# A gated pair of S4 convolutions on one core: cheaper seeds, gates and Dskip, and u's transform split 64 x 32

## The chip, the cores and the metric

The kernel runs on one NeuronCore of a Trainium2 chip. The metric is device time in microseconds of one execution, from the runs' own timer; the profile's span (first to last instruction) is about 2 us shorter. The engines are PE (matmul, with its weight loads listed as PEld), DVE (vector), ACT (activation functions and copies), POOL (a second elementwise engine) and SP, which issues DMAs. Each has its own instruction queue, worked off strictly in order; they meet through semaphores.

## The reference

Two state space layers, A and B, each with 512 channels and 128 complex states, filter the same input u (2048 x 512), and a gate per time step mixes the results:

```python
P = exp(dt * A[:, :, None] * l)                  # 512 x 128 states x 2048 steps, complex
K = einsum("dn,dnl,dn->dl", C, P, dt * B).real   # one kernel of 2048 taps per channel
y = irfft(rfft(u, 4096) * rfft(K, 4096))[:2048] + u * Dskip   # causal convolution
g = sigmoid((u * gate_w).sum(-1, keepdims=True))
out = g * y_A + (1 - g) * y_B
```

## The kernel before, in words

All arithmetic is fp32. The 512 channels are worked in 8 chunks (c) of 64; a chunk holds both layers, so 128 columns. The kernel K of a chunk comes in 8 groups of 16 columns: 64 table steps T in all.

*Preparation.* `exp_dt` and `prep` (three groups of chunks: 0, then 1 to 3, then 4 to 7) turn A, B, C and dt into a magnitude, a phase and their logarithms per state and column. PE transposes them with a diagonal matrix, built from an identity in the constant tile `small`.

*Seeds and tables.* `seed(c)` fills two small tiles per chunk: `ml` (exp of al times 0..7 and times 0, 8, .. 56) and `mh` (exp of al times 0, 256, .. and 0, 64, 128, 192), one ACT instruction of 128 columns for every power, 25 a chunk, with the column of ones set by memset once. `seed_angles` does the phases on POOL. Each `tables(T)` multiplies seeds into magnitudes `mr` (POOL, some on DVE) and angles `ang` (POOL), takes sines on ACT (`s`, `sq`), makes `ei` and `mr` real and imaginary parts on DVE, and then PE's `kgen` (L593) contracts over the states: 32 matmuls, each with 32 weight columns in one of four column tiles of PE and 64 columns moved. ACT or DVE copies the 64 x 4 taps from PSUM to `kt`. After every second step POOL adds Dskip (tile `dsk`, zero except in the rows of tap 0) to tap 0 in `kt` (L599), and `first` (L610) begins the transform of the pair.

*Transforms.* A length of 2048 is split as 32 rows (stride 64) times 64. `first` contracts over the 32 rows for four column groups at once, 16 matmuls of 64 weight columns by 128 moved, and writes `xa` or `xb`; `spectrum` (L623) contracts over the 64 with full 128 x 128 matmuls whose weights `w2` (2 MB) stay in SBUF. u goes through the same two functions, in four batches (`u_spectra`, 4 calls of `first` and 8 of `spectrum` each), and its spectrum is stored to DRAM (`us`). `conv` multiplies the spectra on DVE, `back` does the inverse (L714, 64 x 64 tiles of PE) and turns the result over DRAM (`z` to `zb` to `f`, for the last chunk to `xa`), and `fin` (L745) does its last matmuls with the gates as weights, copies to `o` (two buffers) and stores.

*Gates.* `gated` lets PE multiply u with `gate_w`, copied to all 128 rows by a broadcast weight (L655, 4 groups), copies the result, applies Tanh once over 2048 columns on ACT, and scales it in place against the transform's cosines: two DVE operations (L671) and one on POOL (L674) for each of four groups. The result `gsi` holds the weights of `fin`.

*Order.* Every operation gets a number as the program is recorded by `Plan`, with engines it may run on. The table `ORDER` lists all numbers in the order in which they are issued (a "b" picks the second engine). So the order on each engine is fixed by hand or by a planner beforehand, not found at run time. Buffers are rings: 4 PSUM banks `c`, 2 `s`/`sq`, 3 `u`, 2 `uin`, 2 `o`. A helper makes each kind of operation, so many of the profile's lines are those of helpers: L276 (tensor_tensor), L286 (scalar_tensor_tensor), L289 (activation), L294 (DMA), L299 and L301 (copies on ACT and on DVE).

Of the kernel before, what the change touches and what calls it, by code (L numbers as in the profile page):

```python
# [45 lines left out]
def constants():  # L46
    f32 = np.float32
    out = {}
    l1, f1, l2, f2 = np.arange(L1), np.arange(F1), np.arange(L2), np.arange(F2)
    b, g1, a, g2 = np.arange(NB), np.arange(G1), np.arange(NA), np.arange(G2)  # L50
# [3 lines left out]
    for q in range(4):  # L54
# [6 lines left out]
    out["w2"] = np.ascontiguousarray(w2.transpose(1, 0, 2)).reshape(128, F1 * 128).astype(f32)  # L61
    ang = 2 * np.pi * ((b[:, None] * (4 * g1[None, :] + 1)) % 256) / 256
# [8 lines left out]
    out["small"] = np.concatenate([w1.reshape(128, 256), si, si / 2, np.eye(128),  # L71
                                   np.full((128, 1), math.pi / 4)], 1).astype(f32)
# [10 lines left out]
4 182 183 2 0 1 186 82 3 18 19 20 21 22 23 25 26 27 28 29 24 30 31 32 33 34 88 35 185b 184 37 38 40 44 36 39 41 42 47 46 76 11  # L83
399 79 369 43 8 9 12 7 45 48 49 51 50 138 187 188b 86 190 191 74 71 72 53 52 193 189b 84 13 367 83 85 87 222 14 16 194 192b 55
54 56 57 91 92 73 58 61 62 75 94 93 95 59 96 60 63 64 65 89 68 67 69 90b 70 98 101 100 99 102 103 105 104 195 223 66 77 370 78
371 373 114 196b 197b 198 374 107 375 199 113 201 224b 10 372 376 377 378 382 97 80 383 384 400 6 385 81 401 202 379 15 226
204 205 106 108 109 207 208 200 203 210 213 209 206 211b 110 225 386 214 380 381 216 217 219 220 111 389 112 115 116 390 121
122 123 124 117 118 119 227 342 230 215 212 221 234 127 126 129 231 387 229 388 228 431 432 235 403 391 404 233 392 393 120
433 402 412 413 232b 414 415 236 237b 250 394 405 251 218 128 125 406 407 408 409 253 259 256 410 254b 257b 416 417 418 260 17
411b 419 420 421 134 136 132 244 247 368 130 141 131 144 137 262 255 252 5 422 142 143 245b 248b 145 146 135 258 133 343 261  # L90
266 148 150 151 149 152 492 495 491 493 494 445 429 443 430 446 444 395 498 434 139 154 163 153 155 164 437 438 423 241 238
239b 140 435 436 424 157 447 242 156 439 440 158 450 159 451 396 397 448 398 449 147 460 425 461 462 463 426 441 428 427 442
263 452 453 160 464 465 264 466 265 454 455 161 473 475 474 476 162 467 267 165 166 468 268 477 478 469 269b 470 171 172 173
174 480 481 1413 499 344 270 240 274 175 249 246 243 176 346 347 271 272b 273b 167 168 169 275 276b 277b 471 479 623 625 627
# [112 lines left out]
def ssm_mix(ctx: ExitStack, tc: tile.TileContext, a, out, dry=False):  # L207
# [641 lines left out]
```

## Time and profile before

| | |
|---|---|
| time, median of 3 runs | 453.33 us (450.59 to 453.42) |
| the profiled execution's own time | 454.36 us |
| its span | 452.3 us |
| busy: PE, DVE, ACT, POOL | 397.1 (88%), 406.6 (90%), 379.6 (84%), 358.6 (79%) us |
| DMA moved | 84.56 MB, mean 187 GB/s |
| mean granted PE clock | 0.991 |

A row of a group names the line, the engine, the operation, its output and inputs with shapes, then the count, the busy time, the mean ns of one, and the idle time of the engine just before with what ended it. In rows of PE a form such as `128*32 128x64` means 128 rows, 32 weight columns, 64 columns moved. A matmul of the code appears as two passes. Busy time of many short overlapping instructions is counted once, so count times mean can be more than the busy time. The chain is the sequence of work and waits followed back from the last instruction.

### The profile page before, as it was taken

What the parts mean: (1) busy time and instruction counts of PE and PEld (TensorE: products, weight loads), DVE (VectorE), ACT (ScalarE), POOL (GpSimd) and SP (SyncE); (2) the same over time, 40 slices, a digit from 0 to 9 for tenths busy, and PEclk for the clock granted to TensorE, in tenths of its full rate; (3) what the DMA queues carried; (4) which work ended last, traced back from release to release, by engine and by line L of the source; (5) the groups of instructions that cost most, each with busy time, mean ns of one, the idle gap of its engine ahead of it and who ended that gap; (6) DMA issues with size and microseconds to landing.
All of it is one profiled execution on the core that took longest, in us unless ns stands there. A gap on an engine that the chain in (4) does not pass through costs nothing.

```text
span 452.3 us, 22101 instructions
## 1 busy us (share of the span) xinstructions
PE 397.1 (88%) x9628; PEld 354.7 (78%) x9628; DVE 406.6 (90%) x517; ACT 379.6 (84%) x656; POOL 358.6 (79%) x328
## 2 busy tenths in 40 slices
PE   5798967899998878998998998988998889989994
PEld 4787866788886767897988888877887778888973
DVE  5899999999989999899999999999999998986720
ACT  3778899999897999899999999999999978884120
POOL 0795968799988789999999899889999998980010
PEclk9979999999999999999999999999999999999999
DMA  6728942738646567577456554674466857756785
GB/s 205 246 80 266 291 157 77 229 86 260 234 142 194 171 195 214 159 227 214 135 163 186 177 158 143 196 233 114 132 193 197 234 170 203 241 156 190 213 245 152
DMA packets 79760, 84.56 MB, mean 187 GB/s; under 512 B 7728, under 2 KB 62256, under 8 KB 79664
## 3 DMA queue, kind: packets, MB, share of 16 engines
q1 hardware_dynamic: 79472, 82.63, 61.3%
q8 instruction: 75, 1.23, 1.1%
q0 software_dynamic: 192, 0.52, 0.3%
q14 instruction: 21, 0.17, 0.1%
HBM read 51.48 MB, written 31.65 MB: 184 GB/s over the span
## 4 chain that ended last, share of the span: by engine, by line
PE 39%; DVE 20%; ACT 17%; issue 10%; DMA 8%; POOL 4%; SPq 1%; DVEq 0%; ACTq 0%; POOLq 0%
PE c L623 11%; PE c L610 10%; PE c L593 6%; DVE mr L286 5%; PE c L745 4%; PE c L714 4%; DVE ei L276 3%; ACT s L289 3%; DVE y L694 3%; ACT ang L289 3%; DMA out_dram<-o 3%; PE c L655 2%; ACT sq L289 2%; DMA zb<-z 2%; ACT L289 2%
## 5 line engine op out<-in xcount | busy, mean ns | idle before, releaser
L286 DVE SCALAR_TENSOR_TENSOR mr<-sq,mr 128x1024 f32<-128x1024 f32 (+1 forms) x128 | 117.0, 949 | 2.7 <-ACT sq L289 2.4
L276 POOL TENSOR_TENSOR mr<-ml 128x1024 f32<-128x1024 f32 x52 | 101.6, 1954 | 9.1 <-PE c L593 6.5
L276 DVE TENSOR_TENSOR ei<-s,mr 128x1024 f32<-128x1024 f32 x64 | 77.8, 1216 | 1.4 <-POOL mr L276 0.6
L593 PE MATMUL c<-mr 128*32 128x64 f32 x2048 | 64.0, 222 | 15.3 <-DVE mr L286 5.3
L276 POOL TENSOR_TENSOR ang<-par,cint 128x512 int32<-128x512 int32 x64 | 67.6, 1057 | 10.1 <-ACT sq L289 10.0
L694 DVE TENSOR_TENSOR y<-c,u 128x1024 f32<-128x1024 f32 x57 | 68.3, 1216 | 3.8 <-PE c L623 2.8
L610 PE MATMUL c<-small,kt 128*64 128x128 f32 x1024 | 64.4, 276 | 7.3 <-issue 3.4
L276 POOL TENSOR_TENSOR mr<-mh 128x512 f32<-128x512 f32 x64 | 68.5, 1075 | 1.1 <-PE c L593 0.8
L289 ACT ACTIVATE s<-ang 128x1024 f32<-128x1024 int32 x64 | 66.1, 1032 | 3.3 <-DVE ei L286 2.6
L276 POOL TENSOR_TENSOR ang<-sa 128x512 int32<-128x512 int32 x64 | 68.6, 1073 | 0.2
L289 ACT ACTIVATE ang<-ang 128x1024 f32<-128x1024 int32 x64 | 67.7, 1058 | 1.2
L289 ACT ACTIVATE sq<-ang 128x1024 f32<-128x1024 f32 x64 | 66.2, 1035 | 2.7 <-DVE mr L286 1.8
L593 PEld LDWEIGHTS c<-mr 128*32 128x32 f32 x2048 | 48.3, 109 | 25.3 <-issue 9.0
L610 PEld LDWEIGHTS c<-small,kt 128*64 128x64 f32 x1024 | 56.0, 137 | 12.3 <-issue 7.0
L593 PE MATMUL c<-ei 128*32 128x64 f32 x2048 | 63.0, 219 | 0.5 <-issue 0.5
L714 PE MATMUL c<-y,vv 64*64 64x128 f32 x1792 | 59.2, 273 | 2.3 <-ACT kt L299 0.7
L714 PEld LDWEIGHTS c<-y,vv 64*64 64x64 f32 x1792 | 50.7, 133 | 8.0 <-issue 2.1
L623 PE MATMUL c<-xa,w 128*128 128x128 f32 x384 | 52.5, 284 | 4.9 <-DVE vv L419 2.2
L623 PEld LDWEIGHTS c<-xa,w 128*128 128x128 f32 x384 | 45.8, 191 | 9.7 <-issue 3.6
L623 PE MATMUL c<-xb,w 128*128 128x128 f32 x384 | 50.5, 282 | 2.7 <-DVE xb L301 1.9
L593 PEld LDWEIGHTS c<-ei 128*32 128x32 f32 x2048 | 50.2, 110 | 0.8 <-issue 0.6
L623 PEld LDWEIGHTS c<-xb,w 128*128 128x128 f32 x384 | 45.2, 191 | 6.3 <-DVE xb L301 1.6
(110 smaller groups left out, 653.4 us busy)
## 6 DMA issues: line engine op xcount, KB each, us to landing
zb<-z SPq DMA_DIRECT2D x64, 256.0 KB, 3.4
u<-us SPq DMA_DIRECT2D x57, 256.0 KB, 3.9
f<-zb SPq DMA_DIRECT2D x112, 128.0 KB, 3.7
us<-z SPq DMA_DIRECT2D x32, 256.0 KB, 3.6
uin<-in_uk_dram SPq DMA_DIRECT2D x16, 256.0 KB, 3.2
f<-in_ut_dram SPq DMA_DIRECT2D x8, 512.0 KB, 5.1
out_dram<-o SPq DMA_DIRECT2D x28, 128.0 KB, 2.6
par<-prd SPq DMA_DIRECT2D x7, 320.0 KB, 4.1
```

The lines of the kernel that those rows point to most:

```text
L276: lambda e: (dve if e == "dve" else pool).tensor_tensor(out=out(), in0=in0(), in1=in1(), op=o),
L286: lambda _: dve.scalar_tensor_tensor(out=out(), in0=in0(), scalar=s, in1=in1(), op0=o0, op1=o1), reads, writes, port=port)
L289: op("act", "act", n, lambda _: act.activation(out=out(), in_=in_(), func=func, **{k: v() if callable(v) else v for k, v in kw.items()}), ...
L593: pe.matmul(ps[32 * j:32 * j + 32, o], x[:, 4 * o + j, 64:96], x[:, 4 * o + j, 0:64], start=part == 0, stop=part == 1, tile_position=(0, 3 ...
L610: pe.matmul(t(*ps[g // 4])[64 * r:64 * r + 64, 128 * (g % 4):128 * (g % 4) + 128], t(*x)[:, g], t("small")[:, 128 * r:128 * r + 128], star ...
L623: pe.matmul(view()[:, :, k], t("w2", j // 2)[:, 4 * (j % 2) + k], t(*x1)[:, 4 * j + k], start=True, stop=True)
L655: pe.matmul(p[:, 2 * n:2 * n + 2], t("gate_w")[:, k:k + 1].to_broadcast([128, 128]), fv(n)[:, :, k], start=k == 0, stop=k == 3)
L694: op("dve", "tt1", 1024, lambda _: dve.tensor_tensor(out=t(*y).rearrange("p h s f d -> p h s (f d)"), in0=fv().rearrange("p s f d -> p s ( ...
L714: pe.matmul(bank_of(x)[64 * e:64 * e + 64, CH * q:CH * q + CH], v[:, 0:64] if h else v[:, 32:96], t(*ys[f // 4])[64 * x:64 * x + 64, h, :, ...
L745: pe.matmul(t(*ps)[64 * r:64 * r + 64, DC * i:DC * i + DC], t("gsi")[:, 4 * k + i, s, 64 * r:64 * r + 64], t(*f)[:, 8 * k + 2 * i + r, DC ...
```

## The change

- *Seeds.* POOL multiplies al with the row 0..7 into `ml` (one operation of 1024 elements), and four ACT instructions make all powers of a chunk from it, three of 1024 and one of 512 elements, written in runs of 8 or 4. The memsets go.
- *Dskip.* After each table step DVE adds `dsk` to the tap 0 that it reads from PSUM, 4 elements a row, and writes it to `kt`, behind the copy. POOL's add after every second step goes.
- *u's transform.* 64 rows (stride 32) times 32. `first_u`: 64 matmuls a call, 32 weight columns in four column tiles, 64 columns moved. `spectrum_u`: 16 matmuls a call for two of the old calls, in 64 x 64 tiles, with weights `w2u` loaded from DRAM for each of four groups of a batch into the ring `u` (16 loads of 256 KB). The order of the frequencies f1 in the constants changes with it.
- *Gates.* PE's product with `gate_w` goes to 32 rows in four column tiles (32 matmuls in two calls), Tanh reads it from PSUM in two calls of 256 columns, four matmuls of 512 columns spread a row to all 128 rows, and DVE makes both halves of `gsi` from PSUM (16 operations of 256 elements). The identity and the cosines lie in `o` for a time.
- *The end.* The last two outputs of the last chunk go to `uin` buffers instead of `o`; the second queue for output DMAs is ACT's, not POOL's.
- *Order.* The whole table `ORDER` is another one. Besides the operations above, 9 copies to `kt`, 8 of the output copies of `fin`, 16 to `xa` and `xb` and 7 to `z` move from DVE to ACT, and two products of tables from POOL to DVE.

At the start of PE's queue the first transforms of u (`uin`) and the second ones (`xb`) stand as follows before; `ei` with `y` or `gsi` are the transposes of the preparation.

```order
L610 MATMUL c<-small,uin 64x128 x16
L444 MATMUL c<-ei,y 128x128 x5
L610 MATMUL c<-small,uin 64x128 x32
L444 MATMUL c<-ei,gsi 128x128 x15
L610 MATMUL c<-small,uin 64x128 x32
L623 MATMUL c<-xb,w_0_195 128x2x64 x8
L623 MATMUL c<-xb,w_1_196 128x2x64 x8
L623 MATMUL c<-xb,w_2_197 128x2x64 x8
```

And so in the changed kernel, where L647 is `first_u` and L664 `spectrum_u`, whose weights lie in `u`:

```order
L647 MATMUL c<-small,uin 32x64 x64
L459 MATMUL c<-ei,y 128x128 x4
L647 MATMUL c<-small,uin 32x64 x64
L459 MATMUL c<-ei,y 128x128
L647 MATMUL c<-small,uin 32x64 x64
L459 MATMUL c<-ei,gsi 128x128 x15
L647 MATMUL c<-small,uin 32x64 x64
L664 MATMUL c<-xb,u 64x2x64 x32
L647 MATMUL c<-small,uin 32x64 x64
L664 MATMUL c<-xb,u 64x2x64 x32
L647 MATMUL c<-small,uin 32x64 x64
```

A call of 16 matmuls became one of 64, 32 matmuls of L664 stand for 16 of the old full-size ones, and six calls of the first transform instead of five stand ahead of the first `kgen`.

In the middle of the program, POOL's queue before holds the Dskip add of a pair among its table products (`kt`, the number names the buffer's instance):

```order
L276 TENSOR_TENSOR mr_3410<-mh_1_194 128x16x32
L276 TENSOR_TENSOR ang_3587<-par_1869,cint_201 128x16x32
L276 TENSOR_TENSOR ang_3587<-sa_2930 128x16x32
L276 TENSOR_TENSOR mr_3594<-mh_1_194 128x16x32
L276 TENSOR_TENSOR kt_3458<-kt_3458,dsk_2630 128x8
L276 TENSOR_TENSOR ang_3598<-par_1869,cint_201 128x16x32
L276 TENSOR_TENSOR ang_3598<-sa_2930 128x16x32
```

In the changed kernel it is DVE's queue that holds two adds for the pair, each reading the bank `c` of its own table step, among the products of tables (`ei`, `mr`) and of the convolution (`y`):

```order
L291 TENSOR_TENSOR ei_3834<-s_3745,mr_3718 128x16x64
L301 SCALAR_TENSOR_TENSOR ei_3834<-s_3745,mr_3718 128x16x32
L743 TENSOR_TENSOR y_3848<-c_3842,u_3821 128x1024
L743 TENSOR_TENSOR y_3862<-c_3857,u_3829 128x1024
L291 TENSOR_TENSOR kt_3840<-c_3748,dsk_3134 128x4
L301 SCALAR_TENSOR_TENSOR mr_3718<-sq_3855,mr_3718 128x16x64
L743 TENSOR_TENSOR y_3954<-c_3866,u_3825 128x1024
L291 TENSOR_TENSOR kt_3840<-c_3871,dsk_3134 128x4
L301 SCALAR_TENSOR_TENSOR mr_3718<-sq_3855,mr_3718 128x16x32
```

The add moved from POOL to DVE and from one per pair to one per step; what stands behind it there are the products `mr` and `y`.

The diff, cut to its core:

```diff
 ORDER = """
-4 182 183 2 0 1 186 82 3 18 19 20 21 22 23 25 26 27 28 29 24 30 31 32 33 34 88 35 185b 184 37 38 40 44 36 39 41 42 47 46 76 11
...
+174 2 4 175 13 14 15 16 17 18 20 21 22 23 24 25 19 26 27 28 0 5 29 80 3 9 178 8 1 182 74 76 75 30 177 31 176 78 32 33 34 39 35
...
-    def dma(size, out, in_, reads, writes, also_pool=False, touch=()):
-        op("sp pool" if also_pool else "sp", "dma", size,
-           lambda e: (sp if e == "sp" else pool).dma_start(out=out(), in_=in_()), reads, writes, touch=touch)
+    def dma(size, out, in_, reads, writes, also_act=False, touch=()):
+        op("sp act" if also_act else "sp", "dma", size,
+           lambda e: (sp if e == "sp" else act).dma_start(out=out(), in_=in_()), reads, writes, touch=touch)
...
-    def seed(c, parts):
+    def seed(c):
         ml, mh = ("ml", c % 2), ("mh", c % 2)
-        cols = [(mh, l, 256 * l) for l in range(1, 8)] + [(mh, 8 + l, 64 * l) for l in range(4)]
-        cols += [(ml, l, l) for l in range(1, 8)] + [(ml, 8 + l, 8 * l) for l in range(1, 8)]
...
-                        act.activation(out=t(*tile)[:, ks, j], in_=t("par", c)[:, 0, ks].bitcast(F32), func=AF.Exp, scale=float(l))
...
+        tt("pool", CH * 8, lambda: t(*ml)[:, :, 0:8], lambda: t("par", c)[:, 0].bitcast(F32).unsqueeze(2).to_broadcast([128, CH, 8]),
+           lambda: t("small")[:, 513:521].unsqueeze(1).to_broadcast([128, CH, 8]), OP.mult, par(c, "al") + [("small",)], q[0])
+
+        def exps(_):
+            x = t(*ml)
+            for o, n, l in ((t(*mh)[:, :, 0:8], 8, 256), (t(*mh)[:, :, 8:12], 4, 64), (x[:, :, 8:16], 8, 8), (x[:, :, 0:8], 8, 1)):
+                act.activation(out=o, in_=x[:, :, 0:n], func=AF.Exp, scale=float(l))
...
+        tt("dve", 4, lambda: t(*kt)[:, 4 * (T % 2):4 * (T % 2) + 4, 0], lambda: t(*kc)[:, 0:256].rearrange("p (o l) -> p o l", o=4)[:, :, 0],
+           lambda: t("dsk", c)[:, g], OP.add, [kc, kt, ("dsk", c)], [kt], port=False)
         if T % 2:
-            tt("pool", 8, lambda: t(*kt)[:, :, 0], lambda: t(*kt)[:, :, 0],
-               lambda: t("dsk", c)[:, g - 1:g + 1].rearrange("p t o -> p (t o)"), OP.add, [kt, ("dsk", c)], [kt])
...
+    def first_u(b, h, x, x1):
...
+            for g in range(16):
+                for r in range(4):
+                    pe.matmul(t(*ps[g // 8])[32 * r:32 * r + 32, 64 * (g % 8):64 * (g % 8) + 64], xv[:, g],
+                              t("small")[:, 256 + 64 * r:320 + 64 * r], start=True, stop=True, tile_position=(0, 32 * r))
...
+    def spectrum_u(b, J, x1):
+
+        w, ps = ("u", "w2u", b, J), [("c", "us", b, 2 * J + x) for x in range(2)]
+        dma(256, lambda: t(*w).rearrange("p h f d -> p (h f d)"), lambda: a["w2u"][:, 512 * J:512 * J + 512], (), [w])
+
+        def mm(_):
+            for m in range(4):
+                for x in range(2):
+                    for e in range(2):
+                        pe.matmul(t(*ps[x])[64 * e:64 * e + 64].rearrange("p (h f d) -> p h f d", h=2, f=4)[:, :, m],
+                                  t(*w)[64 * x:64 * x + 64, e, m], t(*x1)[64 * x:64 * x + 64, 8 * J + 4 * e + m],
+                                  start=True, stop=True, tile_position=(64 * x, 64 * e))
...
+                for k in range(4):
+                    for n in range(4):
+                        pe.matmul(t(*ps)[32 * n:32 * n + 32, 0:256].rearrange("p (i l) -> p i l", i=2),
+                                  t("gate_w")[:, k:k + 1].to_broadcast([128, 32]), fv(n)[:, :, k], start=k == 0, stop=k == 3,
+                                  tile_position=(0, 32 * n))
...
+            actv(256, lambda P=P: t(*gt)[:, 4 * P:4 * P + 4].rearrange("p a l -> p (a l)"), lambda ps=ps: t(*ps)[:, 0:256], AF.Tanh,
+                 [ps], [gt] * (P == 0) + [("tanh", P)], table=0, scale=0.5, touch=[gt] * (P > 0))
...
+                pe.matmul(t(*ps), t("small")[:, 521 + n:522 + n].to_broadcast([128, 128]), t(*gt).rearrange("p a l -> p (a l)"),
+                          start=True, stop=True)
...
+                        dve.scalar_tensor_tensor(
+                            out=t("gsi")[:, 8 * P + 2 * n:8 * P + 2 * n + 2, s],
+                            in0=t(*ps)[:, 256 * P:256 * P + 256].rearrange("p (i l) -> p i l", i=2), scalar=1.0,
+                            in1=t("o", "si").rearrange("p a l -> p (a l)")[:, 128 * s:128 * s + 128].unsqueeze(1).to_broadcast([128, 2, 128]),
+                            op0=o, op1=OP.mult)
...
-        f, ps, o = home(c), ("c", "fin", c, k), ("o", c, k)
+        late = c == NCH - 1 and k >= 2
+        f, ps, o = home(c), ("c", "fin", c, k), ("uin", "late", k) if late else ("o", c, k)
```

More of the change, by code (lines that the diff above doesn't have):

```diff
@@ L61, in constants @@
     out["w2"] = np.ascontiguousarray(w2.transpose(1, 0, 2)).reshape(128, F1 * 128).astype(f32)
+    g = (f1.reshape(4, 2, 1, 4).transpose(1, 0, 2, 3) + F1 * np.arange(2)[:, None]).reshape(2, F1)
+    ang = 2 * np.pi * ((np.arange(64)[:, None, None] * (4 * g + 1)) % 256) / 256
+    c, s = np.cos(ang), np.sin(ang)
+    w1u = np.zeros((2, 64, 2, 2, F1, 2))
+    for q in range(2):
+        w1u[q, :, :, 0, :, q] = c
+        w1u[q, :, :, 1, :, q] = -s
+    k = np.arange(32)[None, :, None, None] * (4 * g[:, None, :, None] + 1 + 256 * g2)
+    ang = 2 * np.pi * (k % 8192) / 8192
+    c, s = np.cos(ang), np.sin(ang)
+    w2u = np.stack([np.stack([c, -s], 4), np.stack([s, c], 4)], 1)
+    out["w2u"] = w2u.reshape(128, F1 * 64).astype(f32)
     ang = 2 * np.pi * ((b[:, None] * (4 * g1[None, :] + 1)) % 256) / 256
@@ L643, in gated @@
     def gated():
-        for h in range(4):
-            ps, w, f = ("c", "rows", h), ("gsi", h), ("f", "gate", h // 2)
-            fv = lambda n, f=f, h=h: t(*f)[:, 16 * (h % 2) + 8 * n:16 * (h % 2) + 8 * n + 8].rearrange("p (i k) l -> p i k l", i=2)
-            for n in range(2):
-                dma(512, lambda n=n, fv=fv: fv(n), lambda n=n, h=h: a["ut"][:, 4 * h + 2 * n:4 * h + 2 * n + 2], (),
-                    [f, ("gated", h, n)])
-            def mm(_, ps=ps, fv=fv):
-                p = t(*ps).rearrange("p (i l) -> p i l", i=4)
-                for n in range(2):
-                    for k in range(4):
-                        pe.matmul(p[:, 2 * n:2 * n + 2], t("gate_w")[:, k:k + 1].to_broadcast([128, 128]),
-                                  fv(n)[:, :, k], start=k == 0, stop=k == 3)
-            op("pe", "gate", 32, mm, [f, ("gated", h, 0), ("gated", h, 1), ("gate_w",)], [ps], table="full")
-            copy(512, lambda h=h: t("gsi")[:, 4 * h:4 * h + 4, 0], lambda ps=ps: t(*ps).rearrange("p (i l) -> p i l", i=4), [ps],
-                 [w] + R(1, "P0", "P1", "P2", "P3", "B0", "B1"))
@@ L661, in gated @@
[L661 to L674 removed]
+        dma(128, lambda: t("o", "si").rearrange("p a l -> p (a l)"), lambda: a["si"], (), [("o", "si")])
@@ new lines, in gated, with mm, scaled @@
+        for n in range(4):
+            ps, w = ("c", "rows", n), ("gsi", n)
+            def mm(_, ps=ps, n=n):
+                pe.matmul(t(*ps), t("small")[:, 521 + n:522 + n].to_broadcast([128, 128]), t(*gt).rearrange("p a l -> p (a l)"),
+                          start=True, stop=True)
+            op("pe", "rows", 8, mm, [("tanh", 0), ("tanh", 1), ("small",)], [ps], table="full", touch=[gt])
+            for s, o in ((0, OP.add), (1, OP.subtract)):
+                def scaled(_, s=s, o=o, ps=ps, n=n):
+                    for P in range(2):
+                        dve.scalar_tensor_tensor(
[3 more added lines that the diff above has]
+                            op0=o, op1=OP.mult)
+                op("dve", "stt2", 512, scaled, [ps, ("o", "si")], [w] + R(1, "P0", "P1", "P2", "P3", "B0", "B1"), port=False)
@@ L764, in ssm_mix @@
     load("cint")
-    load("small", 257)
+    load("small", 263)
+    dma(64, lambda: t("o", "eye").rearrange("p a l -> p (a l)")[:, 0:128], lambda: a["eye"], (), [("o", "eye")])
     load("gate_w")
     memset("dummy", lambda: t("dummy"))
-    for k in range(2):
-        for n, j in (("mh", 0), ("ml", 0), ("ml", 8)):
-            memset(n, lambda n=n, j=j, k=k: t(n, k)[:, :, j], *((n, k, q) for q in range(CH // QK)))
     for k in range(4):
@@ L775, in ssm_mix @@
     prep(0)
-    seed(0, ((0, CH),))
+    seed(0)
     seed_angles(0, ((0, 32), (32, 96)))
```

170 lines of the change are left out of this document (75 added, 95 removed), and 49 rows, old and new, of the table ORDER.

## The prediction

> **What bounds the kernel now.** I read the table of stretches first (busy time of each engine), then the chain of waits, then the groups of instructions, and last the single rows of the chain at the start and at the end. The columns of the stretches are length, then busy us of PE, PE's weight loads, DVE, ACT and POOL, the granted clock, the DMA share and GB/s.
>
> ```profile
> core 0: us, PE busy (x) PEld busy (x) DVE busy (x) ACT busy (x) POOL busy (x), PEclk, DMA share, GB/s
> 0.00:30.00 30.00, 21.88 (x201) 19.84 (x202) 23.26 (x63) 18.88 (x42) 14.58 (x22) 0.89 0.59 183
> 30.00:60.00 30.00, 25.74 (x429) 24.17 (x430) 28.78 (x39) 25.07 (x53) 24.42 (x23) 1.00 0.87 258
> ...
> 100.00:140.00 40.00, 38.89 (x888) 34.65 (x882) 38.62 (x46) 37.23 (x55) 37.34 (x34) 1.00 0.69 216
> ...
> 410.00:437.00 27.00, 26.72 (x681) 24.77 (x682) 14.62 (x17) 7.41 (x15) 0.92 (x2) 1.00 0.74 212
> 437.00:452.00 15.00, 9.51 (x140) 6.04 (x138) 1.21 (x4) 1.16 (x3) 1.62 (x3) 0.96 0.62 184
> ...
> 30.00:410.00 380.00, 338.94 (x8608) 304.03 (x8608) 367.46 (x437) 352.16 (x597) 341.45 (x302) 1.00 0.62 186
> ...
> PE 39%; DVE 20%; ACT 17%; issue 10%; DMA 8%; POOL 4%; SPq 1%; DVEq 0%; ACTq 0%; POOLq 0%
> ```
>
> The reader should see three stages. From 30 to 410 us all four engines are nearly full, DVE most of all: 367.46 of 380, 96.7%, against 92.7% for ACT and 89-90% for POOL and PE. After 410 PE works alone; after 437 the end waits for transfers. The chain jumps between engines (PE 39%, DVE 20%, ACT 17%), so nothing is won by relieving one engine only; in the middle the time follows DVE's load as long as the others lose as much.
>
> **ACT, part by part.** The seeds, the table loads and the copies out of PSUM have these rows (busy us, mean ns of one):
>
> ```profile
> L528 ACT ACTIVATE ml<-par 128x128 f32<-128x128 f32 x112 | 29.4, 431 | 0.1
> L528 ACT ACTIVATE mh<-par 128x128 f32<-128x128 f32 x88 | 23.8, 439 | 0.1
> L528 ACT ACT_TABLE_LOAD x12 | 15.4, 1283 | 0.2
> L289 ACT ACTIVATE s<-ang 128x1024 f32<-128x1024 int32 x64 | 66.1, 1032 | 3.3 <-DVE ei L286 2.6 <-POOL ang L276 0.5
> L299 ACT ACTIVATE z<-c 128x512 f32<-128x512 f32 x67 | 38.0, 593 | 7.8 <-PE c L623 3.4 <-DMA zb<-z 1.7 <-PE c L714 1.5
> L299 ACT ACTIVATE kt<-c 128x256 f32<-128x256 f32 x45 | 17.2, 381 | 7.3 <-PE c L593 7.3
> L289 ACT ACTIVATE gsi<-gsi 128x2048 f32<-128x2048 f32 x1 | 1.9, 1912 | 0.0
> ```
>
> Removed: 200 exponentials, 29.4 + 23.8 = 53.2; table loads fall from 29 to 21 in the instruction order, 8 x 1.283 = 10.3; the Tanh 1.9 and two copies of gates 1.2: 66.6. Added: eight seeds of three 1024-wide and one 512-wide pass, 8 x (3 x 1.032 + 0.593) = 29.5. The new order also gives ACT copies that were DVE's: 23 more of 512 at 0.593, 19 more of 256 at 0.381 (two of these are the new Tanh), one of 384 at about 0.5: 21.3. Net -15.8. [...]
>
> **DVE.**
>
> ```profile
> L301 DVE COPY z<-c 128x512 f32<-128x512 f32 x21 | 14.0, 683 | 3.1 <-DMA f<-zb 2.0 <-PE c L714 0.8 <-PE c L623 0.3
> L301 DVE COPY kt<-c 128x256 f32<-128x256 f32 x19 | 7.8, 418 | 1.7 <-PE c L593 1.5
> L671 DVE SCALAR_TENSOR_TENSOR gsi<-gsi,small 128x256 f32<-128x256 f32 x8 | 8.0, 1057 | 0.0
> L286 DVE SCALAR_TENSOR_TENSOR ea<-ea,er 128x8 f32<-128x8 f32 x6 | 1.0, 167 | 0.2
> L276 DVE TENSOR_TENSOR mr<-c,ml 128x1024 f32<-128x1024 f32 x12 | 14.6, 1217 | 0.4 <-PE c L593 0.3
> ...
> L671 DVE SCALAR_TENSOR_TENSOR gsi<-gsi,small x8: 411/840/2169, 134.4 to 158.0; 128x256 f32<-128x256 f32 x8
> ```
>
> Removed: 25 copies of 512, 17.1; a net 17 of 256, 7.1; one of 384, 0.5; the old gate scaling 8.0: 32.7. Added: 16 gate operations of 256 elements. The last row (minimum, median, maximum) shows 0.411 for one that nothing held up, and the new ones read PSUM and one SBUF operand instead of two: 16 x 0.411 = 6.6. Two table products come over from POOL, 1.2 + 0.7. The 64 Dskip adds of 4 elements have no row; the nearest are DVE's own 8-element operation (0.167) and POOL's old add (0.222, below), so 10.7 to 14.2. I take 0.18, near DVE's own: 11.5. Net -12.7, between -13.5 and -10.0.
>
> **POOL.**
>
> ```profile
> L276 POOL TENSOR_TENSOR mr<-ml 128x1024 f32<-128x1024 f32 x52 | 101.6, 1954 | 9.1 <-PE c L593 6.5 <-POOL kt L276 0.8 <-ACT s L289 0.6
> L276 POOL TENSOR_TENSOR kt<-kt,dsk 128x8 f32<-128x8 f32 x32 | 7.1, 222 | 14.0 <-ACT kt L299 11.5 <-ACT z L299 2.1 <-DVE kt L301 0.2
> L276 POOL TENSOR_TENSOR gsi<-small,gsi 128x512 f32<-128x512 f32 x4 | 5.1, 1284 | 0.0
> L332 POOL MEMSET ml<- 128x128 f32 x4 | 1.1, 341 | 0.0
> L294 POOL DMA_DIRECT2D out_dram<-o x4 | 2.3, 586 | 26.9 <-ACT o L299 22.8 <-DVE o L301 4.2
> ```
>
> Removed: 7.1, 5.1, six memsets 2.0, the two products that are now DVE's (1024 and 512 wide, 1.954 and about 1.0) 3.0, four output issues 2.3: 19.5. Added: eight products of 1024 for the seeds at 1.954: 15.6. Net -3.9, the smallest relief of the four. But POOL also loses the 14.0 us in which it stood before its own Dskip adds.
>
> **PE.** From the chain, whole bursts back to back (start, us), then one group of the warming matmuls and one row of weight loads:
>
> ```profile
> 35.61 1.03 PE c L593 x64
> 42.12 1.99 PE c L610 x32
> 95.56 3.65 PE c L655 x16
> 99.21 1.90 PE c L610 x32
> 104.06 1.09 PE c L623 x8
> 130.21 1.91 PE c L714 x64
> ...
> L758 PE MATMUL c<-w,w 128*128 128x512 f32 x12 | 5.4, 602 | 0.0
> ...
> 35.62 0.19 PEld L593 LDWEIGHTS c<-ei 128*32 128x32 f32 x8
> ```
>
> Every matmul of the code is two passes in the trace. The first transform of u was 32 passes in 1.90 to 1.99 us; it becomes 128 passes of kgen's form (32 weight columns in four column tiles, 64 columns moved), of which 64 take 1.03: 2.06, so 16 calls cost 1.1 to 2.6 more; I take +2. The second was 32 x 1.09 = 34.9; it becomes 512 passes of the inverse's form (64x64 tiles, 128 columns moved), 64 in 1.91: 15.3, so -19.6. The gates were 4 x 3.65 = 14.6; in four column tiles two calls of 32 passes are a quarter of the 64 passes' time, 3.65, plus eight 512-wide passes at 5.4/12 = 0.45, 3.6: -7.3. Net -25.
>
> [...]
>
> **Start, end, transfers.** At the start the first seeds now need a POOL product (1.95) before four passes (3.7) in place of 25 exponentials at 53.2/200 = 0.27 each (6.7), and DVE does fewer copies ahead of the first preparation. These cancel within 1 us either way: 0. At the end the output copies wait for slots of o:
>
> ```profile
> 437.34 3.18 DMA out_dram<-o
> ...
> 441.28 4.68 DMA out_dram<-o
> ...
> 447.02 2.09 DMA out_dram<-o
> ```
>
> Two of the last four outputs now go to free slots, and output issues leave POOL for ACT, so 3.18 and 4.68 no longer hold the copies; what is late next is the arrival of the last pieces of xa, whose 12 issues end near 442. That leaves 1 to 3 us of gain; I take 2. The 16 loads of the new weights are 4.2 MB more. Eight stand early; at the 258 GB/s and share 0.87 of 30 to 60 us one of 256 KB costs 0.88 us of all engines, 7 us together, of which 4 us stand free in that stretch. They cost nothing while the first transforms cover them, and up to 3 us otherwise.
>
> **The sum.** The middle shrinks by DVE's 12.7 (its share stays near 97%; ACT loses 15.8 and PE 25, POOL's 3.9 plus its lost waits up to 17.9); the end by 2: 14.7. The profiled execution took 454.36 us (span 452.3 and 2.06 around it): 439.7. The median of the runs is 453.33, 1.03 below it, so I predict 439 us, with 433 to 446 for this case alone (DVE's net from -10.0 to -13.5, the end 1 to 3, the loads 0 to 3, and some slack either way).
>
> **Rivals.** *PE frees more than DVE's own load.* PE has 39% of the chain; DVE waits for it as here:
>
> ```profile
> DVE y L694 <- PE c L623: 5.5, 6, 2.0
> ```
>
> With this and like waits gone a further 6 to 8 us go: about 431. For it: 38.89 of 40 busy in 100 to 140, where u and the gates lie. Against: DVE is idle for only 12.5 us in the whole middle. 13%.
>
> *POOL becomes the bound.* Only its -3.9 and the end's -2 remain, 447.5. For it: all others lose more. Against: its 14.0 us of waits for Dskip go too. 11%.
>
> *The new order is looser than the old.* Every instruction has a new place in a fixed order; if the gaps take back what the sum gives, 450 to 453. Nothing in the trace of before can exclude that. 11%.
>
> *The Dskip adds hold DVE.* This is the one on the other side. The 64 adds stand in DVE's fixed order behind ACT's copy of kt; behind each are queued the products of the next tables and of the convolution, for which PE and ACT wait, and the add now also reads the matmul's bank, so that one of the four PSUM banks stays held until DVE comes to it. POOL's 32 adds waited 14.0 us, 0.44 each. It decides from 12.7/64 = 0.20 us of waiting per add; at POOL's 0.44 it is 28 us on the fullest engine: 439 + 28 = 467. Against: the order puts products of other tables between the matmuls and the add. 8%.
>
> *Weight loads of the first transform aren't hidden.* Each group of eight then costs 0.13 + 0.19 = 0.32 instead of 0.13, a call 5.1 us, 16 calls 49 us more on PE and 24 us net; 11 of them stand ahead of the eighth table, where PE is part of the chain: 453 + 20 = 473. The kgen rows speak against it. [...] 3%.
>
> **How the numbers follow.** The first case has 54%. One per cent is about what a measurement of this kernel can tell from no change: below 448.8 is faster, above 457.9 slower. Faster: 54 + 13 + 7 of POOL's 11 = 74%. Same: the other 4 and the looser order's 11 = 15%. Slower: 8 + 3 = 11%. The range from 429 to 452 leaves out the two slow cases and the ends of two others, together under 20%.
>
> **What would show it.** In the changed profile: ACT near 364 busy, DVE 394, POOL 355, PE 372; a burst of the first transform of u in 2.0 to 2.1 us, of the second 32 passes in 0.95; a seed in 3.7; DVE still at 96% or more of the middle; no wait of an output copy for a transfer over 3 us. The prediction is wrong if DVE's idle time in the middle rises by more than 6 us (waits for ACT's kt or for PE name the cause), if POOL passes 95% of it, or if ACT's seed passes take well over 1.03 us for their strided writes.

## The result, and the profile after

| | before | changed |
|---|---|---|
| time, median | 451.96 us (447.84 to 453.42) | 467.94 us (466.68 to 477.58) |
| ratio to before | | 1.034, 95% interval 1.029 to 1.040 |
| profiled execution's own time, span | 454.36, 452.3 us | 468.06, 466.3 us |
| busy: PE, DVE, ACT, POOL | 397.1, 406.6, 379.6, 358.6 us | 388.5, 389.9, 362.9, 355.2 us |

The change made the kernel 16 us slower; the forecast was 14 us faster. (One of its four runs took 477.58 us at a granted clock of 0.956, where the others had 0.971 to 0.978, and is left out of the ratio.) Every engine does less work than before, and three of the four sums came out within 5 us. So the time went into waiting. The page of the changed kernel says on which engine (its busy line, its queue of instruction fetches, its chain, and the group of u's new first transform with its weight loads):

```profile
PE 388.5 (83%) x11428; PEld 341.8 (73%) x11428; DVE 389.9 (84%) x548; ACT 362.9 (78%) x520; POOL 355.2 (76%) x288
...
q8 instruction: 90, 1.47, 1.3%
...
PE 44%; ACT 14%; issue 14%; POOL 12%; DVE 8%; DMA 6%; SPq 1%; DVEq 0%; ACTq 0%; POOLq 0%
...
L647 PE MATMUL c<-small,uin 128*32 128x64 f32 x2048 | 38.9, 238 | 25.4 <-issue 15.2
...
L647 PEld LDWEIGHTS c<-small,uin 128*32 128x32 f32 x2048 | 35.1, 122 | 26.1 <-issue 19.1
```

The page before had this line for the same queue:

```profile
q8 instruction: 75, 1.23, 1.1%
```

"issue" in the chain grew from 10% to 14%: time in which PE waited for nothing that the profile shows. The list of waits of the changed kernel (engine, line, releaser: us in total, times, longest) has it at the top, and behind it the engines that wait for PE:

```profile
PEld c L647 <- issue: 19.1, 11, 5.2
PEld c L605 <- issue: 17.6, 35, 1.7
POOL mr L291 <- PE c L605: 15.4, 9, 4.4
PE c L647 <- issue: 15.2, 9, 3.5
...
ACT xb L314 <- PE c L647: 14.2, 5, 6.9
ACT kt L314 <- PE c L605: 12.2, 18, 2.4
...
ACT xa L314 <- PE c L647: 11.9, 4, 4.6
```

Where it happens is seen in the stretches. First the changed kernel, then two rows of before. The middle is taken from 30 us to the last table product of POOL, which ends at 418.2 after and at 405.7 before:

```profile
30.00:60.00 30.00, 18.65 (x846) 15.65 (x841) 22.53 (x33) 20.96 (x34) 20.79 (x17) 0.95 0.81 243
60.00:100.00 40.00, 28.66 (x917) 25.90 (x912) 36.18 (x51) 36.81 (x51) 33.19 (x25) 0.84 0.55 178
...
220.00:260.00 40.00, 28.65 (x1079) 25.58 (x1075) 25.61 (x34) 26.75 (x40) 27.03 (x22) 0.96 0.50 142
...
30.00:418.00 388.00, 329.36 (x9944) 290.77 (x9939) 350.85 (x468) 336.39 (x477) 343.44 (x271) 0.97 0.64 191
```

```profile
220.00:260.00 40.00, 36.93 (x975) 34.07 (x964) 38.03 (x50) 39.16 (x69) 37.98 (x32) 1.00 0.59 173
...
30.00:406.00 376.00, 335.36 (x8526) 300.87 (x8529) 363.55 (x433) 348.89 (x594) 341.45 (x302) 1.00 0.62 186
```

DVE's load in the middle fell by 12.7 us (363.55 to 350.85), exactly the forecast, but its idle time rose from 12.5 to 37.2 us, so the middle grew by 12. Most of the loss lies in two places, 30 to 60 us and 220 to 260 us, where u's batches are transformed: there DVE is idle for 6.3 and 12.4 us more than before. In the second, all four engines are idle for 28 to 36% of the time. The chain of waits of the changed kernel there, in order of time (start, us, what):

```profile
231.38 1.94 PE c L647 x128
...
236.81 0.89 PE c L647 x63
237.71 3.50 issue
241.21 1.93 PE c L647 x64
243.14 1.66 PE c L605 x64
244.80 1.96 PE c L647 x127
246.76 2.53 issue
...
251.41 1.47 PE c L647 x94
252.88 1.83 issue
```

A burst of 128 passes does take 1.94 to 1.96 us, as forecast. But inside three of these four calls (128 passes each) PE stops, for 1.83 to 3.50 us, and waits for nothing that the profile shows. The first theory is therefore that PE lacks instructions. A call of `first_u` is 64 matmuls of two passes, each a weight load and a matmul: 256 instructions, where the old call of 16 had 64. The queue of fetches moved 1.47 MB in 90 packets for 2 x 11428 instructions of PE, 254 to a packet of 16 KB, and two such packets never followed each other in less than 3.29 us in this trace. One call uses up in 2.0 us about what one packet holds, and the packets start 3.3 us apart at best.

Work behind a pause ran at half clock in some places. `kgen` (L605) takes 1.66 us at 243.14, shortly behind the pause of 3.50 us, where 64 passes took 1.03 before; the granted clock is one half from 241.21 to 244.62. The clock was also halved behind a pause of only 1.91 us (17 passes of L664 took 1.33 us at 57.56, where 32 took 1.10 at 65.09), and not behind the one of 2.53 us (L622 took its usual 1.90). No run here shows what halves it. The 0.84 of 60 to 100 us, where it was 1.00 before, can't be laid to instructions alone: PE's waits at the halved stretches there include 2.39 and 1.93 us for copies of ACT (up to 73.50 and 87.41) and 2.16 us for a table angle of POOL (up to 97.92).

### The profile page after: what moved, and what is told of

The parts are those of the page before. It is cut to its first block, busy times and chain, and to the rows that moved or that the text cites. A ratio compares the mean times of both kernels' runs of the same rounds, so it can differ in the third digit from the quotient of the medians.

```text
span 466.3 us, 25524 instructions
## 1 busy us (share of the span) xinstructions
PE 388.5 (83%) x11428; PEld 341.8 (73%) x11428; DVE 389.9 (84%) x548; ACT 362.9 (78%) x520; POOL 355.2 (76%) x288
## 3 DMA queue, kind: packets, MB, share of 16 engines
q8 instruction: 90, 1.47, 1.3%
## 4 chain that ended last, share of the span: by engine, by line
PE 44%; ACT 14%; issue 14%; POOL 12%; DVE 8%; DMA 6%; SPq 1%; DVEq 0%; ACTq 0%; POOLq 0%
PE c L605 9%; PE c L622 8%; PE c L763 6%; PE c L635 6%; PE c L647 6%; POOL ang L291 5%; POOL mr L291 5%; PE c L796 4%; ACT ang L304 3%; ACT s L304 2%; ACT sq L304 2%; DVE mr L301 2%; DVE y L743 2%; DMA u<-us 2%; ACT z L314 2%
## 5 line engine op out<-in xcount | busy, mean ns | idle before, releaser
L291 POOL TENSOR_TENSOR mr<-ml 128x1024 f32<-128x1024 f32 x51 | 99.7, 1955 | 22.1 <-PE c L605 15.4
L605 PE MATMUL c<-mr 128*32 128x64 f32 x2048 | 68.0, 227 | 16.7 <-issue 4.7
L605 PEld LDWEIGHTS c<-mr 128*32 128x32 f32 x2048 | 50.6, 113 | 26.0 <-issue 14.1
L622 PE MATMUL c<-small,kt 128*64 128x128 f32 x1024 | 64.4, 279 | 4.7 <-ACT vv L314 2.4
L605 PE MATMUL c<-ei 128*32 128x64 f32 x2048 | 66.7, 224 | 1.6 <-issue 1.5
L763 PE MATMUL c<-y,vv 64*64 64x128 f32 x1792 | 61.3, 273 | 5.2 <-issue 3.8
L622 PEld LDWEIGHTS c<-small,kt 128*64 128x64 f32 x1024 | 56.9, 139 | 11.6 <-issue 5.6
L647 PE MATMUL c<-small,uin 128*32 128x64 f32 x2048 | 38.9, 238 | 25.4 <-issue 15.2
L605 PEld LDWEIGHTS c<-ei 128*32 128x32 f32 x2048 | 52.5, 113 | 3.5 <-issue 3.4
L647 PEld LDWEIGHTS c<-small,uin 128*32 128x32 f32 x2048 | 35.1, 122 | 26.1 <-issue 19.1
L314 ACT ACTIVATE z<-c 128x512 f32<-128x512 f32 x75 | 42.8, 591 | 11.7 <-PE c L763 7.4
L301 DVE SCALAR_TENSOR_TENSOR ei<-s,mr 128x512 f32<-128x512 f32 x64 | 43.5, 679 | 0.0
```

What stands on the lines that cost most here:

```text
L291: lambda e: (dve if e == "dve" else pool).tensor_tensor(out=out(), in0=in0(), in1=in1(), op=o),
L301: lambda _: dve.scalar_tensor_tensor(out=out(), in0=in0(), scalar=s, in1=in1(), op0=o0, op1=o1), reads, writes, port=port)
L314: act.activation(out=o(), in_=i(), func=AF.Copy)
L605: pe.matmul(ps[32 * j:32 * j + 32, o], x[:, 4 * o + j, 64:96], x[:, 4 * o + j, 0:64], start=part == 0, stop=part == 1, tile_position=(0, 3 ...
L622: pe.matmul(t(*ps[g // 4])[64 * r:64 * r + 64, 128 * (g % 4):128 * (g % 4) + 128], t(*x)[:, g], t("small")[:, 128 * r:128 * r + 128], star ...
L647: pe.matmul(t(*ps[g // 8])[32 * r:32 * r + 32, 64 * (g % 8):64 * (g % 8) + 64], xv[:, g], t("small")[:, 256 + 64 * r:320 + 64 * r], start= ...
```

## The experiments

Theory 1 is this supply of instructions. Theory 2 is the rival "the new order is looser", theory 3 the rival "the Dskip adds hold DVE". A first set takes u's transforms apart, a second the supply by itself, a third Dskip, a fourth asks where the rest of the gain is.

### u's transforms: undone, and put into the kernel before

The first kernel is the changed one with u's transforms of before, all else and the order of all else as changed:

```diff
-            first_u(b, h, i, x1)
+            first(("u", b, h), i, x1, 32 * h)
...
-                spectrum_u(b, j // 2, x1)
+                for i in (j, j + 1):
+                    spectrum(x1, i, ...)
```

> The changed kernel with u's two transforms as they were before (16 matmuls of 64 weight columns a call, then full-size ones with resident weights) and everything else, the order too, as changed. Theory 1, PE's instruction supply: in the changed trace the packets of PE's instruction queue, 256 instructions each, are never closer than 3.3 us, and u's new first transform uses 256 instructions in 2.0 us, so PE runs dry; with 64 instructions a call instead of 256 PE's idle time put to issue falls from about 90 us (rows of PE and its loads) toward the 50 of before, and the time is 440 to 452 us, although PE has some 20 us more matmul work. Theory 2, the new order is looser than the old one: 462 us or more. Theory 3, the Dskip adds on DVE hold the PSUM banks: 464 to 470 us, no change.

Measured: 447.36 us against 451.24, ratio 0.990 (0.982 to 0.997). u's new transforms cost 20.6 us of the 468; the rest of the change gains 4, a small gain whose interval just leaves out no change. It keeps the order and the Dskip adds, so neither theory 2 nor theory 3 can be the main cause.

The second is the kernel before in which only u's first transform becomes 64 narrow matmuls of as many products. Its transform of u is not the reference's.

```diff
+            if many:
+                xv = t(*x).rearrange("p a (b l) -> p (a b) l", l=32)
+                for g in range(16):
+                    for r in range(4):
+                        pe.matmul(t(*ps[g // 8])[32 * r:32 * r + 32, ...], xv[:, g], t("small")[:, 64 * r:64 * r + 64], ...)
+                return
...
-            first(("u", b, h), i, x1, 32 * h)
+            first(("u", b, h), i, x1, 32 * h, True)
```

> The kernel before, in which only the matmuls of u's first transform are replaced by 64 of 32 weight columns and 64 moved columns a call; same banks, same copies, same order. The spectrum of u, and so the output, is not the reference's. PE's matmul work grows by about 2 us. Theory 1 (instruction supply): 3072 more instructions, 12 blocks of at least 3.3 us, for the most part in stages where PE is waited for: 460 to 470 us. Theories 2 and 3: 451 to 455 us.

Measured: 477.70 us, ratio 1.058 (1.050 to 1.065), more than the 460 to 470 of theory 1; what the excess is made of stays open. The order is that of before, so theory 2 can't explain it. The waits of this kernel, where L612 is the first transform of u:

```profile
PEld c L593 <- issue: 17.4, 26, 2.4
PEld c L612 <- issue: 15.8, 10, 3.2
PE c L612 <- issue: 15.6, 9, 3.0
```

The third is the changed kernel with 16 wide matmuls in `first_u` (the reverse edit; the spectrum of u is not the reference's), the second transform and its loads as changed.

> The changed kernel, in which only the matmuls of u's first transform are replaced by 16 of 64 weight columns and 128 moved columns a call; second transform, banks, copies and order stay as changed. The spectrum of u, and so the output, is not the reference's. Theory 1 (instruction supply): PE's issue waits in u's first transform go from 34 us to under 8, the time falls to 436 to 450 us. Theory 2 (looser order) and theory 3 (Dskip adds): 462 to 470 us.

Measured: 451.51 us, ratio 1.002 (0.998 to 1.006), just above the range given. The narrow first transform alone is worth 16.4 us. What is left against the first kernel, 4.1 us, belongs to the second transform in quarter tiles with its 16 loads: it lowered PE's busy time by 8.3 us (390.3 to 382.0) and yet lost time. Why was not taken apart further.

### The supply by itself

The next kernel has nothing of the reference's computation, only PE on operands that stand in SBUF: 32 matmuls of 512 columns, 1024 of kgen's narrow form, 16 of 512 columns, 512 of 64 weight columns by 128 moved, 32 of 512, and the narrow 1024 again beside stores.

> PE alone, nothing of the reference's computation: 32 matmuls of 128x128 weights by 512 columns, then 1024 of kgen's form (32 weight columns in four column tiles, 64 columns moved, so 4096 instructions in the trace), 16 wide ones, 512 of the inverse's form (64x64 tiles, 128 columns moved, 2048 instructions), 16 wide ones, and the 1024 narrow ones once more while 64 stores of 512 KB run. All operands stand in SBUF and nothing waits for another engine. Theory 1 (instruction supply): the narrow passes start at about 16 ns each, as in kgen's bursts, and fall to about 27 ns once the instructions fetched ahead are used up, that is 256 instructions per 3.3 to 3.6 us, with idle time put to issue in steps of about 1.5 us per 128 passes; the first 2048 narrow passes take 45 to 56 us in place of the 33 that the bursts' pace gives. The half form needs 30 ns a pass in the trace of before and stays near that, 1024 passes in 30 to 34 us. If the stores slow the fetches, the last 2048 narrow passes take longer than the first. Rival (the form itself, not its supply, is slow, because its weight loads are not hidden over a long run): an even pace above 27 ns from the first pass, with no idle time put to issue. Rival (other engines in the full kernel, not the instructions): 2048 narrow passes in 33 us, without gaps.

PE's timeline (start, us, line, passes, idle before and its releaser), L245 being the narrow form and L251 the wider one:

```profile
4.84 30.14 PE L240 MATMUL p<-w 128*128 128x512 f32 x64 [4.84 <-DMA w<-in_w_dram]
34.91 2.44 PE L245 MATMUL p<-small,w 128*32 128x64 f32 x159
38.61 1.99 PE L245 MATMUL p<-small,w 128*32 128x64 f32 x128 [1.26 <-issue]
...
77.97 1.99 PE L245 MATMUL p<-small,w 128*32 128x64 f32 x128 [1.46 <-issue]
81.43 1.99 PE L245 MATMUL p<-small,w 128*32 128x64 f32 x128 [1.46 <-issue]
84.88 1.99 PE L245 MATMUL p<-small,w 128*32 128x64 f32 x128 [1.46 <-issue]
...
103.75 56.12 PE L251 MATMUL p<-small,w 128*64 128x128 f32 x1024
...
241.26 3.64 PE L245 MATMUL p<-small,w 128*32 128x64 f32 x128 [1.46 <-issue]
246.36 1.99 PE L245 MATMUL p<-small,w 128*32 128x64 f32 x128 [1.46 <-issue]
```

This shows the pauses by themselves. After 159 passes, PE runs nearly throughout in steps of 128 passes, 256 instructions: 1.99 us of work, 1.46 us of nothing, one step per 3.45 us (some steps took up to 4.0). The 2048 passes took 55 us (34.9 to 89.9) where the burst's pace gives 33. The page's row of DMA traffic in 40 slices of 7 us shows what flows meanwhile:

```profile
GB/s 112 0 0 0 0 5 5 5 5 5 5 5 5 2 0 2 2 2 2 2 2 2 2 0 0 370 404 401 397 402 402 399 407 405 403 406 382 45 302 299
```

5 GB/s in the narrow stretch is 16.4 KB per 3.45 us (4.7), with every other queue silent; 2 GB/s where the wider form runs, without a pause; nothing under the 512-wide ones. Beside stores of 400 GB/s, the steps come every 5.1 us or a little more (241.26 to 246.36), and in many the work lasts up to 3.64 us, at a granted clock of 0.72 in the mean from 194 to 265 us. The trace ties the pauses to the packets one by one. Each of the 28 pauses of over 1 us in this kernel ends 2.2 to 2.9 us after a packet of the instruction queue has started. The changed kernel's three pauses above do the same: they end at 241.21, 249.29 and 254.71, which is 2.25, 2.50 and 2.41 us after packets that started at 238.96, 246.79 and 252.30. In the supply kernel PE works off 256 instructions in 1.99 us, and in most steps the next 256 start 3.45 us after the last.

One expectation was wrong: the wider form was called the inverse's and given 30 ns a pass. It took 54.8; it has 128 rows and so is the form of the old first transform, for which the prediction's rows show 32 passes in 1.90.

### Dskip

The changed kernel with its 64 adds moved to POOL, at the same places of the order:

```diff
-        tt("dve", 4, ..., lambda: t(*kc)..., lambda: t("dsk", c)[:, g], OP.add, [kc, kt, ("dsk", c)], [kt], port=False)
+        tt("pool", 4, ..., lambda: t(*kt)..., lambda: t("dsk", c)[:, g], OP.add, [kt, ("dsk", c)], [kt], port=False)
```

> The changed kernel with the 64 Dskip adds on POOL (4 elements, from kt to kt) instead of DVE, at the same places of the order. Theory 3 (the adds hold DVE and the banks): 10 us or more faster, under 458 us. Theories 1 and 2: 464 to 472 us, since DVE stood only 1.5 us before these adds in the trace and POOL gets about 13 us of work.

Measured: 512.68 us, ratio 1.138 (1.128 to 1.148), a miss for every theory. Its waits:

```profile
POOL kt L291 <- ACT kt L314: 45.8, 21, 5.6
DVE ei L291 <- POOL mr L291: 37.1, 21, 5.4
```

POOL's queue stands behind ACT's copy, and DVE behind POOL's products. The wait behind ACT's copy that the rival feared for DVE shows here, on POOL. On DVE the adds cost almost nothing, as the next kernel shows: the first kernel (447.36 us) with the adds left out of the program, so without u times Dskip.

> The changed kernel with the old transforms of u (measured at 447.4 us), and the 64 Dskip adds on DVE left out of the program, so that the output lacks u times Dskip. They are 64 x 0.156 = 10.0 us of DVE's busy time. If DVE's own load still sets the middle, as the prediction has it, the time falls by 8 to 11 us, to 436 to 439. If the new order is looser, so that DVE waits for others anyway, most of the 10 us becomes waiting: 443 to 447. Theory 1 alone says nothing of this run; it asks where the 8 us lie that the kernel with the old transforms lacks against the forecast of 439.

Measured: 446.29 us, ratio 0.988 (0.984 to 0.992), 1 us. Theory 3 falls. It also says that in this version DVE's load no longer sets the time; 443 to 447 was what the expectation gave for a looser order. Part of the reason is in the busy times: the adds' row is 9.9 to 10.1 us, but without it DVE is busy for 385.6 us against 390.3, only 4.7 less (4.3 in the last pair below, 389.2 to 384.9). The adds overlap their neighbours: the trace of the changed kernel has its first adds start 0.08 us before the end of the operation ahead.

### Where the rest of the gain is

With u's transforms undone, the change gains 4 us, not 14.7. The next kernel takes POOL's seed products of six chunks out of that version; the exponentials then work on what stands in the tile, with the sign of their factors turned.

> The changed kernel with the old transforms of u (447.4 us), with POOL's seed products left out for six of the eight chunks (the exponentials then work on what stands in the tile, so tables are wrong): 6 x 1.95 = 11.7 us of POOL's busy time, which stood at 341.6 of 376 us of the middle (91%). If POOL has become the bound there, the time falls by 8 to 12 us, to 436 to 439. If DVE is still the bound, or the order's gaps are, it stays at 445 to 448.

Measured: 448.74 us, ratio 0.991 (0.986 to 0.996): no gain over 447.36. Then `kgen` itself, whose 32 narrow matmuls are 128 instructions a table step, in the version with the old transforms and in the kernel before:

```diff
-            for o in range(4):
+            for o in range(2):
                 for x, part in ((R, 0), (I, 1)):
-                    for j in range(4):
-                        pe.matmul(ps[32 * j:32 * j + 32, o], x[:, 4 * o + j, 64:96], x[:, 4 * o + j, 0:64], ...)
+                    for j in range(2):
+                        pe.matmul(ps[64 * j:64 * j + 64, 2 * o:2 * o + 2], x[:, 8 * o + 4 * j, 0:64],
+                                  x[:, 8 * o + 4 * j:8 * o + 4 * j + 2, 0:64], ...)
```

> The changed kernel with the old transforms of u (447.4 us), and kgen's 32 matmuls of 32 weight columns by 64 moved replaced by 8 of 64 weight columns by 128 moved, the form of the old first transform (32 passes in 1.90 to 1.99 us, so 16 passes in about 0.97 us against 1.03). The taps are no longer the reference's. PE's busy time hardly changes, but a table step issues 32 instructions instead of 128: 6144 fewer of some 19300, 24 fetches of 256 fewer. Theory 1 widened (the supply of PE's instructions holds the middle in every version, and that is where the gain forecast went): 10 to 20 us less, 427 to 437 us. Rival (the supply holds PE only in the bursts of u's new first transform; elsewhere the order's gaps take the gain): 443 to 448 us.

> The kernel before with the same 8 wide matmuls in kgen instead of 32 narrow ones; the taps are not the reference's. Theory 1 widened: the supply also holds the kernel before, whose middle needs 70 fetches in 380 us, 5.3 us apart, and 24 fewer of them take 6 to 15 us off, 436 to 445 us. Rival (before, the fullest engine, DVE with 97% of the middle, sets the time, and the supply has slack): 448 to 453 us. If this run stays and the run of the changed kernel with the same edit falls, the supply took the gain of the other engines; if both stay, it is the order.

Measured: 436.89 us, ratio 0.968 (0.962 to 0.974), and 447.11 us, ratio 0.992 (0.987 to 0.996). PE's busy time hardly moved (385.2 against 390.3, and 392.1 against 397.1), the fetches fell from 76 to 52 and from 75 to 51. The first falls in the range of theory 1; the second lies above its 436 to 445 and just under the rival's 448. So the supply holds the version with the old transforms outside u's bursts too, though PE's 5 us less of busy time could account for about half of its 10 us. In the kernel before 3 us were gained, and there PE's busy time alone may account for them. With the wide `kgen` in both, the rest of the change is worth 10.2 us (447.1 to 436.9), most of the 14.7 forecast. Two rows of the first of the two:

```profile
140.00:180.00 40.00, 38.23 (x740) 33.81 (x738) 39.91 (x53) 38.12 (x56) 39.92 (x32) 1.00 0.64 188
...
260.00:300.00 40.00, 37.17 (x677) 32.82 (x678) 39.80 (x53) 38.04 (x53) 39.92 (x32) 1.00 0.62 186
```

DVE and POOL both stand at 99.5% or more there. The same wide `kgen` beside u's new transforms asks whether the total of the instructions counts or their density:

> The changed kernel with u's new transforms as they are (64 narrow matmuls a call), and kgen's 32 narrow matmuls replaced by 8 wide ones; the taps are not the reference's. PE now has some 16700 instructions, fewer than the 19256 of the kernel before. If the total of the instructions is what counts, it comes near the run with the old transforms and the same edit, 434 to 441 us. If it is their density, 256 in a call of 2.0 us against a supply of 256 per 3.5 us, each of the 16 calls still runs dry by about 1.5 us, and part of these 23 us stays: 445 to 458 us. Rival (a looser order alone): 458 to 468 us.

Measured: 450.84 us, ratio 0.999 (0.995 to 1.002), 14 us above the version with the old transforms (some 4 of them the second transform's, by the third kernel), though PE has fewer instructions (16712) than in the kernel before (19256). Density counts; the waits of this kernel still show it, L648 being `first_u`:

```profile
PEld c L648 <- issue: 14.5, 13, 5.3
ACT xb L314 <- PE c L648: 14.3, 6, 6.7
```

Last, whether DVE or POOL is the bound once the instructions come in time: the version of 436.89 us without the Dskip adds, and without six of POOL's seed products.

> The changed kernel with the old transforms of u and 8 wide matmuls in kgen (436.9 us), and the 64 Dskip adds on DVE left out too (10.0 us of its busy time); taps wrong, no u times Dskip. With the narrow kgen the same omission gave 1 us. If the supply stood in the way there and DVE is the bound without it, the time now falls by 7 to 10 us, to 427 to 430 us. If the order's gaps hold both, it stays at 434 to 437 us.

> The changed kernel with the old transforms of u and 8 wide matmuls in kgen (436.9 us, 0.968 of the kernel before), and POOL's seed products left out for six of the eight chunks, 11.7 us of its busy time; the tables and taps are wrong. With the narrow kgen the same omission gave nothing (448.7 against 447.4). In the run of 436.9 us POOL was busy for 39.3 to 40.0 of 40 us in five stretches between 100 and 380 us. If POOL is the bound once the instructions come in time, the time falls by 6 to 11 us, a ratio of 0.944 to 0.955. If no single engine is, but the order that couples them, it stays within 3 us, 0.961 to 0.972.

Measured: 437.10 us, ratio 0.968 (0.962 to 0.973), and 438.26 us, ratio 0.968 (0.962 to 0.974). Neither gains. The stretch from 100 to 380 us of the two runs, in the same order:

```profile
100.00:380.00 280.00, 261.98 (x4770) 233.55 (x4769) 273.01 (x313) 262.31 (x377) 274.88 (x217) 1.00 0.67 197
```

```profile
100.00:380.00 280.00, 261.36 (x4750) 232.75 (x4748) 275.24 (x363) 262.03 (x375) 264.47 (x213) 1.00 0.67 197
```

With DVE relieved, POOL is still busy for 98% of it, and with POOL relieved, DVE is. So neither is the only bound, and relieving one engine gains nothing, as the prediction's first part said of the kernel before. No run relieved both; whether the two together or the fixed order hold this version at 437 us stays open.

## Why the prediction was wrong

- **PE, first transform of u: the step that failed.** "it becomes 128 passes of kgen's form ... of which 64 take 1.03: 2.06, so 16 calls cost 1.1 to 2.6 more". The burst's pace was right (1.94 to 1.96 us), but it came from a burst of 128 instructions that stands among others, and was used for 256 in a row, several calls behind one another. The supply kernel puts one burst per 3.45 us in its place. The row of L647 sums to 38.9 us of busy time where 16 bursts of 2.06 give 33, and the narrow form costs 16.4 us of the kernel's time where the sum has +2 of PE's busy time. No bound of the term held this, since nothing in the sum priced an instruction as such.

The groups of the changed kernel that answer to the other terms:

```profile
L664 PE MATMUL c<-xa,u 64*64 64x128 f32 x256 | 11.6, 305 | 4.0 <-issue 3.0 <-DVE z L316 0.5 <-ACT z L314 0.5
L664 PE MATMUL c<-xb,u 64*64 64x128 f32 x256 | 10.1, 276 | 2.5 <-ACT xb L314 0.8 <-ACT z L314 0.8 <-issue 0.5
...
L711 PE MATMUL c<-uin,small 128*128 128x512 f32 x8 | 4.4, 631 | 0.0
...
L700 PE MATMUL c<-f,gate_w 128*32 128x256 f32 x64 | 3.9, 381 | 0.0
```

```profile
L541 ACT ACTIVATE ml<-ml 128x1024 f32<-128x1024 f32 x16 | 16.8, 1050 | 0.3
```

```profile
L291 DVE TENSOR_TENSOR kt<-c,dsk 128x4 f32<-128x4 f32 x64 | 9.9, 156 | 1.5 <-ACT kt L314 1.0
```

- **PE, second transform and gates.** 34.9 to 15.3 was forecast for the second; its rows now sum to 21.7 (L664), and 32 passes take 1.36 in the mean, not 0.95: 1.10 at full clock (at 65.09), 1.99 at half (at 60.68). The gates came as forecast (8.3 against 7.3). PE's sum was 388.5, not 372.
- **ACT, DVE, POOL.** 362.9, 389.9 and 355.2 against 364, 394 and 355: right. The seeds' passes of 1024 took 1.05 us each (L541), 0.02 over the 1.03 taken from the sines' rows, so the strided writes cost no more than that can show. The Dskip adds took 0.156 each, not 0.18, and 0.07 of DVE's busy time.
- **"The middle shrinks by DVE's 12.7 (its share stays near 97%; ...)".** This is the second step that failed. The load shrank so, the share fell to 90%. The clause "the time follows DVE's load as long as the others lose as much" fails twice: PE lost busy time and got later, and even with u's old transforms the adds' 4.7 us of DVE's busy time, taken out, gave 1.
- **The end's 2 us.** The last outputs no longer wait over 3 us for a slot, as foretold. But from POOL's last table product to the end it took 46.6 us before (405.7 to 452.3) and takes 48.1 (418.2 to 466.3). This was not tested.
- **The rivals.** "PE frees more than DVE's own load" came out the other way: PE's busy time fell, but the others wait for PE longer. The slower side had the wrong mechanisms; that the 467 and 473 of its two rivals lie near the 467.94 measured is luck. Dskip: refuted. Weight loads of the first transform not hidden: the rows of before speak against it (eight loads of `kgen` last 0.19 us, while 64 of its passes take 1.03, so eight take 0.13), and the supply kernel refutes it over a long run, 128 passes with as many loads of all 128 rows in 1.99 us, 15.5 ns a pass. It pointed at the right instructions for another reason. POOL as the one bound: refuted by two runs. The looser order is not excluded as part of the missing 4 us.
- **The signs.** The prediction named itself wrong if DVE's idle time rose by over 6 us, with the waits for PE as the cause. It rose by 25, and they were: in the middle its waits for PE are 25.9 us, where they were 5.8 before. The longest of them:

```profile
DVE xa L316 <- PE c L647: 7.1, 2, 3.9
DVE kt L316 <- PE c L605: 7.1, 4, 4.6
DVE y L743 <- PE c L635: 5.3, 7, 1.7
DVE ei L291 <- PE c L605: 3.7, 3, 2.7
```

## What to carry to other kernels

Count PE's instructions beside its passes: two passes of a narrow matmul with a weight load each are four instructions, and in these runs 256 came per 3.3 to 3.45 us at best, per 5.1 us beside stores of 400 GB/s. Where a stretch wanted them faster than that for long, PE stopped: 9 times in the 16 calls of the changed kernel, 15.2 us in all. A rewrite that saves work by four times as many small matmuls should therefore stand where PE has slack in its instructions, spread between long ones, not in calls behind one another; that spreading them helps is argued from these rates, and no run here tried it. "issue" in the chain and in PE's waits, and the packets of the instruction queue, are where a profile shows it.

## What was not expected of the hardware

The instructions of PE came in packets of 16 KB, one per 3.45 us in most steps alone and one per 5.1 us beside stores of 400 GB/s. Both kernels come near this pace: their 75 and 90 packets lie 5.3 and 4.7 us apart in the median. Behind some pauses the granted clock was one half: 64 passes of `kgen` behind one of 3.50 us took 1.66 us in place of 1.03. Behind one of 2.53 us it was not halved, behind one of 1.91 us it was, so the length alone does not decide it here.
